# A value sum with 256 columns: four key tiles and 512 queries a period, and the maxima closed at a period's end

## The chip, the cores and the metric

The kernel runs on one core of a Trainium2 chip. The metric is the device time of one execution in microseconds; each kernel is run several times and the median counts. The engines are named as the profile names them: PE (TensorE, with its weight loads as PEld), DVE (VectorE), ACT (ScalarE), POOL (GpSimd) and SP (SyncE, which here only issues DMAs).

## The reference

One token sequence of 2048 rows with 512 columns goes through two branches, softmax attention with 32 heads of 16 columns and a gated feed-forward layer of width 1792, and a sigmoid gate mixes the two:

```
q, k, v = split(x @ wqkv)                      # 32 heads of 16
a = concat_h(softmax(q_h k_h^T / 4) v_h) @ wo
b = (sigmoid(x @ w_gate) * (x @ w_up)) @ w_down
g = sigmoid(sum(x * gate_w))
out = g * a + (1 - g) * b
```

All inputs and the output are fp32.

## The kernel before

**Number formats.** Most products run in a reduced fp32 format (fp32r): a number is split into a high and a low part, and three products are added (`terms`). The value sum (`values`) is plain fp32, and the profile shows two matmul rows for each of its matmuls.

**Stages.** The kernel projects q and k for the first head pairs, then v, while it already computes the first maxima (`first_max`). Then comes the main loop of NPER = 256 periods. Behind it stand the rest of the feed-forward layer and the output product (`whole_run`, `heads_out`).

**A period** handles one step of three works that are interleaved by hand:

- *t*, exponentials (`st_part`, L457): a matmul gives 128 keys x 512 queries of the logits of one head; the 64 rows it contracts hold q and k parts and the row maximum to subtract. ACT takes the exponential into a tile `p` (L470). There are eight a period: two key tiles, two blocks of 512 queries, two heads. Head 0 of two periods runs in an even period, head 1 of two in an odd one.
- *m*, maxima (`sm_step`, L242): for a head pair that comes later, a matmul gives 128 queries x 512 keys (L255) and DVE reduces each row to its maximum (L257). There are eight a period as well.
- *d*, dense (`dense`, class `Sum`): half matmuls (64 contracted rows) of the q, k, gate and up projections, 12 a period. A run of 24 fills bank `dn` in two periods; ACT evicts it (L317).

Head 0's matmuls and the dense half `d0` use the lower 64 rows of the array, head 1's and `d1` the upper. Neighbouring words of the two halves run at once, so the 28 matmuls stand in 14 pairs. At the end of the period `values(k)` (L475) multiplies the exponentials with v: eight matmuls of 512 columns, in which four blocks of 17 output rows (two heads, two query blocks) lie side by side in the array's columns. ACT evicts the sum (L487), and POOL adds it to the sum over the earlier key tiles (L498); after eight periods the sum goes to DRAM (`pv_d`).

**What sets the order.** `STEADY` (L540) lists the words t, m and d of an even and an odd period. Each engine executes its own list strictly in the program's order. Three things limit PE: the array, the banks and the semaphores. Of eight PSUM banks `dn` belongs to the dense work; the other seven go to t, m and the value sum. The table `REUSE` (L542) says for each of the 34 takes of two periods how many takes ago its bank was last taken; that user's reader (ACT for a t or a value sum, DVE for an m) must be done first. Worked through the table, the value sum takes the bank of the period's fifth m in both kinds of period, and the last m that of the fifth t. The last ten periods (`LAST`) have no m.

**Closing the maxima.** When a head has all 32 maxima of 1024 queries, DVE reduces them to eight columns at once (L261). `split_max` (L265) splits these on POOL; two m words later (`DELAY`) `turn_max` (L271) transposes them on DVE (L275), and SP writes them to DRAM and copies them into the rows of `QS` that the t matmuls of that half read (L276, L280). In the steady stage both heads of a pair close in the same odd period, once in eight periods; the first t that needs a half comes two periods or more after.

`turn` (L154) is a token on POOL between the dense halves, behind an even period's words. `logits` (L452) computes the gate's logits on DVE in 16 of the periods.

Of the kernel before, what the change touches and what calls it, by code (L numbers as in the profile page):

```python
# [12 lines left out]
F32 = mybir.dt.float32  # L13
# [12 lines left out]
P = 128  # L26
# [8 lines left out]
KR = 64  # L35
# [2 lines left out]
NSTEP = NPAIR * 32  # L38
NPER = NSTEP // 2
TAIL = FIRST // 2  # L40
DELAY = 2
LOW, UP = 0, 1


# [1 line left out]
def gated_mix(ctx, tc, x, xc, wqk, wv, wo, w_gu, w_down, gate_w, out):  # L46
# [25 lines left out]
    pv_d = dram.tile([2, NPAIR, P, 512], F32, name="pv_d")  # L72
    rec_d = dram.tile([P, 512], F32, name="rec_d")
    m_d = dram.tile([NPAIR, 2, 2, P, 32], F32, name="m_d")

    warm = keep.tile([P, 1], F32, name="warm")
    dve.memset(warm, 0.0)
# [143 lines left out]
    square = ring(keep, 2, [P, 2, 16], "mhl")  # L221
# [13 lines left out]
    xr.update((c, load_x(c)) for c in range(1, NC))  # L235

    stat = {}
    mrow = {}

    count = {}  # L240

    def sm_step(j):  # L242

        p, s = divmod(j, 32)
        qt, kh = divmod(s, 2)
        qs, ks = QS[p % 2], KS[p % 2]

        def one(b, i):
            half = (p, qt // 8, b)
            if half not in stat:  # L250
# [4 lines left out]
            pe.matmul(t, qs[r:r + KM, qt * P:(qt + 1) * P], ks[r:r + KM, g * 512:(g + 1) * 512],  # L255
                      start=True, stop=True)
            dve.tensor_reduce(stat[half][:, qt % 8, g:g + 1], t, axis=AX.X, op=ALU.max)  # L257
            count[half] += 1
            if count[half] == 32:
                m = keep.tile([P, 8], F32, name=f"m{p}_{qt // 8}_{b}", tag="m", bufs=2)  # L260
                dve.tensor_reduce(m, stat.pop(half), axis=AX.X, op=ALU.max)  # L261
                mrow[half] = m
        return one

    def split_max(half):  # L265
        hl = square()
        split(hl[:, 0, :8].bitcast(F32R), hl[:, 1, :8].bitcast(F32R), mrow.pop(half), pool, pool)
        left = iter(range(DELAY))
        turning.append((lambda: next(left, None) is None, half, hl))

    def turn_max():  # L271
        _, half, hl = turning.pop(0)
        p, i, b = half
        mt = keep.tile([P, 32], F32, name=f"mt{p}_{i}_{b}", tag="mt", bufs=2)
        dve.transpose(mt, hl.rearrange("p a t -> p (a t)"))  # L275
        sp.dma_start(m_d[p, i, b], mt)  # L276
        rows = m_d[p, i, b].rearrange("(g a t) j -> a t g j", g=4, a=2)
# [5 lines left out]
    turning = []  # L283

    wd = []

# [31 lines left out]
    fill = filling()  # L318


    first = [(j, i) for j in [*range(0, 16, 2), *range(1, 16, 2), *range(16, FIRST + 1)] for i in range(2)]

    def first_max():
        if first:
            j, i = first.pop(0)
            if j < FIRST:
                sm_step(j)(0, i)
                sm_step(j)(1, i)
            else:
                for j in range(FIRST, FIRST + 2):  # L330
                    sm_step(j)(1, i)

    for c in range(NC):
        if c + 1 < NC:
# [34 lines left out]
    for t in range(2, NS, 2):  # L369
        two = [Sum(bankv(), tokens(t + a)) for a in range(2)]  # L370
        for g in (LOW, UP):
            first_max()
            for m in range(3 * KT):
                two[0].half(g)
                two[1].half(1 - g)
                if m in (5, 11):
                    first_max()
                if turning and turning[0][0]():
                    turn_max()
                for half in list(mrow):  # L380
                    split_max(half)
# [57 lines left out]

    def denominators(i):  # L440
        rows = slice(64 * i, 64 * i + 64)
        sp.dma_start(den[rows, :], pv_d[i].rearrange("p (c r) q -> (p c) r q", r=32)[:, DH, :])
        dve.reciprocal(den[rows, :], den[rows, :])
        sp.dma_start(rec_d[rows, :], den[rows, :])

# [10 lines left out]

    def st_part(k, b):  # L457

        p, r = divmod(2 * k, 32)
        i, kt = divmod(r, 16)  # L460
        qs, ks = QS[p % 2], KS[p % 2]
        r = 64 * b
        pt = ptile[k, b] = mid(f"p{k}_{b}")
        for a in range(2):
            for c in range(2):
                o = bank()
                q0 = i * 1024 + c * 512
                pe.matmul(o, ks[r:r + KR, (kt + a) * P:(kt + a + 1) * P], qs[r:r + KR, q0:q0 + 512],  # L468
                          start=True, stop=True)
                act.activation(pt[:, 2 * a + c, :], o, AF.Exp, scale=DH ** -0.5)  # L470
                yield

    sums = {}

    def values(k):  # L475

        o = bank()
        half = divmod(k // 8, 2)
        pts = [ptile.pop((k, b)) for b in range(2)]
        for a in range(2):  # L480
            for c in reversed(range(4)):
                h = 2 * half[0] + c // 2
                pe.matmul(o[32 * c:32 * c + VW, :], v[:, 2 * k % 16 + a, h * VW:(h + 1) * VW],  # L483
                          pts[c // 2][:, 2 * a + c % 2, :], start=(a == 0), stop=(a == 1))

        def put(e):
            act.activation(e, o, AF.Copy)  # L487

        if half not in sums:
            sums[half] = keep.tile([P, 512], F32, name=f"sum{half[0]}_{half[1]}", tag="sum", bufs=2)  # L490
            put(sums[half])
        else:
            e = keep.tile([P, 512], F32, name=f"part{k}", tag="part", bufs=2)
            put(e)
            later.append(lambda s=sums[half]: add(s, e))

        def add(s, e):
            pool.tensor_tensor(s, s, e, ALU.add)  # L498
            if k % 8 == 7:
                sp.dma_start(pv_d[half[1], half[0]], s)  # L500

    def mx(b):
        for j in range(FIRST + 2 * b, NSTEP):
            one = sm_step(j)
            for i in range(2):
                one(b, i)
                yield
# [17 lines left out]
    def emit(order, **parts):  # L525

        for word in order.split():
            if word == "turn":
                turn(run)
            elif word == "work":  # L530
                work(1)
            else:
                next(parts[word], None)
                if word[0] == "m":
                    if turning and turning[0][0]():
                        turn_max()
                    for half in list(mrow):
                        split_max(half)

    STEADY = ("t0 m1 d1 m0 t0 d1 d1 m0 t0 d1 t0 d1 d1 m0 d1 work m0 t0 d1 t0 d1 d1 t0 m1 t0 d1 m0 d1 m0",  # L540
              "t1 m0 t1 d0 d0 m1 t1 d0 d0 m1 d0 m1 t1 d0 work m1 d0 t1 d0 d0 t1 m1 m0 t1 d0 d0 t1 d0 m1")
    REUSE = (7, 5, 8, 6, 9, 7, 7, 6, 8, 6, 8, 6, 8, 7, 7, 6, 8,  # L542
             7, 7, 7, 7, 7, 7, 7, 6, 8, 7, 7, 7, 7, 6, 8, 6, 8)
# [13 lines left out]
    for k in range(NPER):  # L557
# [6 lines left out]
        if 128 <= n < 256 and n % 16 in (6, 8):  # L564
            logits((n - 128) // 16 * 2, (n % 16 - 6) // 2)
        if n % 32 == 0 and n // 32 + 1 < NPAIR:
            load_pair(n // 32 + 1)
        if k >= NPER - TAIL:
# [5 lines left out]
        if k >= NPER - TAIL and turning:  # L574
            turn_max()
        emit(STEADY[k % 2] if k < NPER - TAIL else LAST[k - NPER], **parts)
        if k == NPER - 1:
            bankd = bank
        if run.done():
# [49 lines left out]
                raws.append(late_raw(*late[1][:2]))  # L629

    def heads_load(u):
        i, c, q0 = u // 4, (u // 2) % 2, (u % 2) * 256
        ot = lp.tile([P, KT, 256], F32, name=f"ot{u}", tag="ot")
        rb = lp.tile([P, KT, 256], F32, name=f"rb{u}", tag="rb")
        heads = pv_d[i].rearrange("p (b c r) q -> (p b) c r q", b=2, c=2)
        recs = rec_d.rearrange("(i h c) q -> i h c q", i=2, c=2)
        for k in range(KT):
            hs = slice(8 * k, 8 * k + 8)
            sp.dma_start(ot[:, k, :], heads[hs, c, :DH, q0:q0 + 256])
            sp.dma_start(rb[:, k, :], recs[i, hs, c, q0:q0 + 256].unsqueeze(1).to_broadcast([8, DH, 256]))  # L640
        return ot, rb

    def heads_split(u, ot, rb):
# [89 lines left out]
```

## Time and profile before

| What | Value |
|---|---|
| median of the runs | 1758.79 us (1758.29 to 1759.24, 3 runs) |
| the profiled execution's own time | 1758.72 us |
| its span | 1756.2 us |
| PE, PEld | 1749.5 us (100%), 1060.2 us (60%) |
| DVE, ACT, POOL | 1422.0 us (81%), 1321.8 us (75%), 478.1 us (27%) |
| main loop, first to last steady period | 96.8 to about 1473 us |
| its last ten periods | about 1473 to 1523 us |
| granted clock of PE | 0.998 |

A row of the timeline gives the start in us from the span's start, the duration in us, the engine, the line, the operation, what it writes and reads, and how many equal rows were merged; in square brackets stands the idle time ahead of it and what ended it. `sm` and `st` are the seven shared banks. A row of the groups gives the total busy time and the mean of one in ns. In the table of windows each engine's busy time is followed by its count.

### The profile page before, as it was taken

The numbers are of one execution on the slowest core, as the hardware profiler recorded it, in microseconds if no ns is written. First come the engines' busy times: TensorE is split into PE (matmuls) and PEld (weight loads), VectorE is DVE, ScalarE is ACT, GpSimd is POOL, SyncE is SP. The second block draws the span as 40 slices with busy tenths as digits, with TensorE's granted clock in tenths as the row PEclk, the third lists the DMA queues.
The fourth block names the chain that finished last, engine by engine and source line by source line (L and its number), as shares of the span: only waits on it lengthen the run. The fifth ranks groups of instructions, "written<-read, shape, count | busy, mean of one in ns | idle before, by whom it ended". The sixth has DMA issues, their size and how long they took to land.

```text
span 1756.2 us, 33183 instructions
## 1 busy us (share of the span) xinstructions
PE 1749.5 (100%) x12676; PEld 1060.2 (60%) x12676; DVE 1422.0 (81%) x2346; ACT 1321.8 (75%) x2564; POOL 478.1 (27%) x501
## 2 busy tenths in 40 slices
PE   9999999999999999999999999999999999999999
PEld 7755555555555555555555555555555555588887
DVE  5988888888998889888888888888888886256543
ACT  4188888888888888888888888888888888944221
POOL 1124343423232313222222222222222222342110
PEclk9999999999999999999999999999999999999999
DMA  9311424241313131413131313122121312367652
GB/s 254 78 37 61 88 68 92 68 104 44 80 56 80 48 75 47 85 51 86 38 74 38 74 36 65 45 59 53 50 63 44 63 44 68 120 227 256 232 191 72
DMA packets 89567, 149.75 MB, mean 85 GB/s; under 512 B 23424, under 2 KB 31616, under 8 KB 86400
## 3 DMA queue, kind: packets, MB, share of 16 engines
q1 hardware_dynamic: 89120, 147.11, 31.2%
q8 instruction: 99, 1.62, 0.4%
q14 instruction: 60, 0.49, 0.1%
q10 hardware_dynamic: 288, 0.52, 0.1%
HBM read 87.56 MB, written 60.03 MB: 84 GB/s over the span
## 4 chain that ended last, share of the span: by engine, by line
PE 99%; DVE 0%; ACT 0%; issue 0%
PE dn L145 19%; PE sm L483 16%; PE sm L468 12%; PE st L483 11%; PE sm L255 10%; PE st L468 9%; PE sm L688 7%; PE st L255 7%; PE st L132 4%; PE dn L688 2%; PE st L145 1%; PE sm L597 1%; PE st L597 1%; PE st L80 0%; DVE stat L257 0%; ACT p L470 0%
## 5 line engine op out<-in xcount | busy, mean ns | idle before, releaser
L257 DVE TENSOR_REDUCE stat<-sm 128x1 f32<-128x512 f32 x1205 | 774.2, 680 | 100.3 <-PE sm L255 87.4
L470 ACT ACTIVATE p<-sm 128x512 f32<-128x512 f32 x1167 | 666.9, 652 | 0.1
L257 DVE TENSOR_REDUCE stat<-st 128x1 f32<-128x512 f32 x843 | 552.0, 679 | 70.9 <-PE st L255 61.9
L470 ACT ACTIVATE p<-st 128x512 f32<-128x512 f32 x881 | 522.2, 652 | 9.2 <-PE st L468 8.6
L498 POOL TENSOR_TENSOR sum<-sum,part 128x512 f32<-128x512 f32 x224 | 289.3, 1291 | 722.8 <-ACT part L487 696.6
L255 PE MATMUL sm<-ks,qs 48*128 48x512 f32 x1205 | 463.7, 419 | 0.2 <-DVE stat L257 0.2
L468 PE MATMUL sm<-qs,ks 64*128 64x512 f32 x1167 | 454.6, 424 | 0.3 <-ACT part L487 0.3
L468 PE MATMUL st<-qs,ks 64*128 64x512 f32 x881 | 351.6, 425 | 1.5 <-ACT v L361 1.4
L255 PE MATMUL st<-ks,qs 48*128 48x512 f32 x843 | 341.8, 419 | 0.0
L468 PEld LDWEIGHTS sm<-qs,ks 64*128 64x128 f32 x1167 | 211.2, 185 | 174.6 <-ACT gu L317 48.5
L483 PE MATMUL sm<-p,v 128*17 128x512 f32 x2384 | 285.1, 595 | 0.0
L255 PEld LDWEIGHTS sm<-ks,qs 48*128 48x128 f32 x1205 | 218.3, 185 | 38.1 <-DVE stat L257 7.8
L468 PEld LDWEIGHTS st<-qs,ks 64*128 64x128 f32 x881 | 161.1, 186 | 130.9 <-ACT gu L317 35.7
L483 PE MATMUL st<-p,v 128*17 128x512 f32 x1712 | 204.6, 595 | 0.0
L255 PEld LDWEIGHTS st<-ks,qs 48*128 48x128 f32 x843 | 155.4, 185 | 25.0 <-DVE stat L257 3.0
L487 ACT ACTIVATE part<-sm 128x512 f32<-128x512 f32 x132 | 81.1, 614 | 107.8 <-issue 92.7
L483 PEld LDWEIGHTS sm<-p,v 128*17 128x17 f32 x2384 | 55.4, 96 | 141.1 <-issue 92.2
L487 ACT ACTIVATE part<-st 128x512 f32<-128x512 f32 x92 | 56.2, 611 | 77.7 <-issue 62.9
L483 PEld LDWEIGHTS st<-p,v 128*17 128x17 f32 x1712 | 39.7, 96 | 100.9 <-issue 66.2
L96 POOL CAST mhl<-m 128x8 fp32r<-128x8 f32 x64 | 12.1, 189 | 272.7 <-DVE m L261 272.7
L432 DVE TENSOR_TENSOR gul<-gul 128x1024 f32<-128x1024 f32 (+1 forms) x30 | 45.9, 1536 | 34.6 <-ACT gul L431 33.4
L317 ACT ACTIVATE gu<-dn 128x512 f32<-128x512 f32 x99 | 69.1, 698 | 0.0
(456 smaller groups left out, 3042.9 us busy)
## 6 DMA issues: line engine op xcount, KB each, us to landing
gu_d<-gu SPq DMA_DIRECT2D x112, 256.0 KB
gul<-gu_d SPq DMA_DIRECT2D x56, 512.0 KB
qs<-q_d SPq DMA_DIRECT2D x90, 128.0 KB
ks<-k_d SPq DMA_DIRECT2D x90, 128.0 KB
pv_d<-sum SPq DMA_DIRECT2D x32, 256.0 KB
q_d<-qe SPq DMA_DIRECT2D x12, 512.0 KB
k_d<-qe SPq DMA_DIRECT2D x12, 512.0 KB
x<-in_xc_dram SPq DMA_DIRECT2D x16, 256.0 KB
```

The lines of the kernel that those rows point to most:

```text
L132: pe.matmul(o, a, b, start=(i == 0), stop=(i == len(ops) - 1))
L145: mm = pe.matmul(self.o, a[rows], b[rows], start=(self.n == 0), stop=(self.n == 2 * len(self.ops) - 1))
L255: pe.matmul(t, qs[r:r + KM, qt * P:(qt + 1) * P], ks[r:r + KM, g * 512:(g + 1) * 512], start=True, stop=True)
L257: dve.tensor_reduce(stat[half][:, qt % 8, g:g + 1], t, axis=AX.X, op=ALU.max)
L317: leave = lambda e, o: act.activation(e, o, AF.Copy)
L432: dve.tensor_tensor(gu[:, 1, a], gu[:, 0, a], gu[:, 1, a], ALU.mult)
L468: pe.matmul(o, ks[r:r + KR, (kt + a) * P:(kt + a + 1) * P], qs[r:r + KR, q0:q0 + 512], start=True, stop=True)
L470: act.activation(pt[:, 2 * a + c, :], o, AF.Exp, scale=DH ** -0.5)
L483: pe.matmul(o[32 * c:32 * c + VW, :], v[:, 2 * k % 16 + a, h * VW:(h + 1) * VW], pts[c // 2][:, 2 * a + c % 2, :], start=(a == 0), stop=(a ...
L487: act.activation(e, o, AF.Copy)
L498: pool.tensor_tensor(s, s, e, ALU.add)
L688: pe.matmul(down[t], a, b, start=(f == 0 and m == 0), stop=(f == NF - 2 and m == 5))
```

## The change

A period now takes four key tiles and 512 queries in place of two key tiles and 1024 queries. It still has eight t, eight m and 12 d words. What changes:

- `values` issues 16 matmuls of 256 columns: four key tiles, two heads, two halves of the 512 queries. Its output has 256 columns in a bank, so the eviction on ACT and the addition on POOL have 256 columns too. A sum is complete after four periods, with three additions; there are 64 sums of half the size, and the layout of `pv_d` and its readers (`denominators`, `heads_load`) follow.
- `STEADY` and `REUSE` are new tables.
- The closing of the maxima moves behind the words of a period: reduce (now L268), transpose (L270) on DVE, then the split on POOL, which now works on the transposed tile of 32 columns, then the DMAs. `DELAY` and `split_max` go.
- Head 1's maxima run 24 steps ahead in place of 22 (`UPPER`); the additional ones are computed in the first stage. The heads now close in two different odd periods of eight.
- The gate's logits stand behind a period's words too, before its value sum.

```diff
-DELAY = 2
+UPPER = FIRST + 4
...
             if count[half] == 32:
-                m = keep.tile([P, 8], F32, name=f"m{p}_{qt // 8}_{b}", tag="m", bufs=2)
-                dve.tensor_reduce(m, stat.pop(half), axis=AX.X, op=ALU.max)
-                mrow[half] = m
+                full.append(half)
...
     def turn_max():
-        _, half, hl = turning.pop(0)
+        half = full.pop(0)
         p, i, b = half
+        m = square()
+        dve.tensor_reduce(m[:, :8], stat.pop(half), axis=AX.X, op=ALU.max)
         mt = keep.tile([P, 32], F32, name=f"mt{p}_{i}_{b}", tag="mt", bufs=2)
-        dve.transpose(mt, hl.rearrange("p a t -> p (a t)"))
-        sp.dma_start(m_d[p, i, b], mt)
+        dve.transpose(mt, m)
+        hl = keep.tile([P, 2, 32], F32R, name=f"mhl{p}_{i}_{b}", tag="mhl", bufs=2)
+        split(hl[:, 0, :], hl[:, 1, :], mt, pool, pool)
+        sp.dma_start(m_d[p, i, b], hl.bitcast(F32))
...
-        for a in range(2):
-            for c in reversed(range(4)):
-                h = 2 * half[0] + c // 2
-                pe.matmul(o[32 * c:32 * c + VW, :], v[:, 2 * k % 16 + a, h * VW:(h + 1) * VW],
-                          pts[c // 2][:, 2 * a + c % 2, :], start=(a == 0), stop=(a == 1))
+        for a in range(4):
+            for b in reversed(range(2)):
+                h = 2 * p + b
+                for i in reversed(range(2)):
+                    r = 64 * b + 32 * i
+                    pe.matmul(o[r:r + VW, :], v[:, 4 * k % 16 + a, h * VW:(h + 1) * VW],
+                              pts[b][:, a, 256 * i:256 * i + 256], start=(a == 0), stop=(a == 3))
...
-    REUSE = (7, 5, 8, 6, 9, 7, 7, 6, 8, 6, 8, 6, 8, 7, 7, 6, 8,
+    REUSE = (8, 7, 7, 7, 7, 7, 7, 6, 8, 7, 7, 7, 6, 8, 6, 8, 7,
...
         emit(STEADY[k % 2] if k < NPER - TAIL else LAST[k - NPER], **parts)
+        while full:
+            turn_max()
+        if 128 <= n < 256 and n % 16 in (4, 8):
+            logits((n - 128) // 16 * 2, (n % 16 - 4) // 4)
```

Two places show what this makes of the engines' lists. The first is PE at the end of an even period and the start of its value sum. Line L255 (now L254) is an m, L468 (now L461) a t, L145 a d, L483 (now L478) the value sum; `waits` names the semaphores that the row waits for. Before:

```order
L468 MATMUL sm_70<-qs_106,ks_107 128x512 [waits DVE_49]
L255 MATMUL st_66<-ks_107,qs_106 128x512 [waits Activation_49]
L255 MATMUL sm_69<-ks_107,qs_106 128x512 [waits DVE_49]
L468 MATMUL sm_71<-qs_106,ks_107 128x512 [waits Activation_49]
L145 MATMUL dn<-xh,g5h 128x512
L145 MATMUL dn<-xl,g5h 128x512
L468 MATMUL st_67<-qs_106,ks_107 128x512 [waits DVE_49]
L145 MATMUL dn<-xh,g5l 128x512
L255 MATMUL st_65<-ks_107,qs_106 128x512 [waits Activation_49]
L483 MATMUL sm_72<-p_1_9198,v 17x512 [waits DVE_49]
```

In the kernel after the change, the same place:

```order
L254 MATMUL st_67<-ks_107,qs_106 128x512 [waits DVE_49]
L145 MATMUL dn<-xl,u5h 128x512
L145 MATMUL dn<-xh,u5l 128x512
L254 MATMUL sm_71<-ks_107,qs_106 128x512 [waits Activation_49]
L461 MATMUL st_67<-qs_106,ks_107 128x512 [waits DVE_49]
L254 MATMUL sm_70<-ks_107,qs_106 128x512 [waits Activation_49]
L478 MATMUL sm_72<-p_1_10262,v 17x256 [waits Activation_49]
L478 MATMUL sm_72<-p_1_10262,v 17x256
L478 MATMUL sm_72<-p_0_10311,v 17x256 x2
L478 MATMUL sm_72<-p_1_10262,v 17x256 x2
```

The value sum waited for a reduce on DVE and now waits for ACT: by the new table it takes the bank of the period's sixth t, in both kinds of period. The last m still waits for the fifth t, and the last t of an even period, beside it, for the fourth m. The order of the last words differs: four m in place of three now stand among the last six users of a bank.

The second place is DVE around the closing of one pair's maxima. L257 (now L256) is the reduce of a matmul's row maxima, L261 (now L268) the closing reduce, L275 (now L270) the transpose. Before:

```order
L257 TENSOR_REDUCE stat_1_1_3873<-st_66 128x1 [waits PE_49]
L261 TENSOR_REDUCE m_1_1_4382<-stat_1_1_3873 128x8 [waits DVE_49]
L257 TENSOR_REDUCE stat_0_1_4387<-sm_71 128x1 [waits PE_49]
L257 TENSOR_REDUCE stat_0_1_4387<-sm_69 128x1 [waits PE_49]
L257 TENSOR_REDUCE stat_0_1_4387<-st_67 128x1 [waits PE_49]
L275 STREAM_TRANSPOSE mt_1_1_4406<-mhl_117 128x32 [waits DMAHW1_49,Pool_49]
L257 TENSOR_REDUCE stat_1_0_3934<-st_66 128x1 [waits PE_49]
L261 TENSOR_REDUCE m_1_0_4413<-stat_1_0_3934 128x8 [waits DVE_49]
```

After the change, around the closing of one head:

```order
L256 TENSOR_REDUCE stat_1_0_4317<-st_65 128x1 [waits PE_49]
L256 TENSOR_REDUCE stat_0_1_4740<-st_66 128x1 [waits PE_49]
L268 TENSOR_REDUCE msq_118<-stat_1_0_4317 128x8 [waits DVE_49]
L270 STREAM_TRANSPOSE mt_1_0_4855<-msq_118 128x32 [waits DVE_49,Pool_49]
L256 TENSOR_REDUCE stat_0_1_4740<-st_67 128x1 [waits PE_49]
```

The closing reduce and the transpose stood apart, between reduces of matmuls of the same period, with the split on POOL between them. Now they stand together behind the last reduce of a period and ahead of the first of the next, and the split comes after them.

More of the change, by code (lines that the diff above doesn't have):

```diff
@@ L220, in gated_mix @@
     act.activation(g1[:, :1], warm, AF.Exp)
-    square = ring(keep, 2, [P, 2, 16], "mhl")
+    square = ring(keep, 2, [P, 32], "msq")
     for _ in range(2):
@@ L318, in gated_mix @@
     fill = filling()
[L321 removed]
+    first = [(j, i) for j in [*range(0, 16, 2), *range(1, 16, 2), *range(16, FIRST), *range(FIRST, UPPER, 2)] for i in range(2)]
     def first_max():
@@ L463, in st_part @@
         pt = ptile[k, b] = mid(f"p{k}_{b}")
-        for a in range(2):
[L465 to L471, printed above, removed]
+        for a in range(4):
+            o = bank()
+            pe.matmul(o, ks[r:r + KR, (kt + a) * P:(kt + a + 1) * P], qs[r:r + KR, c * 512:(c + 1) * 512],
+                      start=True, stop=True)
+            act.activation(pt[:, a, :], o, AF.Exp, scale=DH ** -0.5)
+            yield
@@ L473, in gated_mix @@
     sums = {}
     def values(k):
-        o = bank()
-        half = divmod(k // 8, 2)
+        o = bank()[:, :256]
+        p, c = part = divmod(k // 4, 4)
         pts = [ptile.pop((k, b)) for b in range(2)]
-        for a in range(2):
-            for c in reversed(range(4)):
-                h = 2 * half[0] + c // 2
-                pe.matmul(o[32 * c:32 * c + VW, :], v[:, 2 * k % 16 + a, h * VW:(h + 1) * VW],
-                          pts[c // 2][:, 2 * a + c % 2, :], start=(a == 0), stop=(a == 1))
@@ L486, in put @@
[L486 to L495, printed above, removed]
+        for a in range(4):
+            for b in reversed(range(2)):
[4 more added lines that the diff above has]
+                              pts[b][:, a, 256 * i:256 * i + 256], start=(a == 0), stop=(a == 3))
@@ L497, in add @@
+        if part not in sums:
+            sums[part] = keep.tile([P, 256], F32, name=f"sum{p}_{c}", tag="sum", bufs=2)
+            act.activation(sums[part], o, AF.Copy)
+        else:
+            e = keep.tile([P, 256], F32, name=f"part{k}", tag="part", bufs=2)
+            act.activation(e, o, AF.Copy)
+            later.append(lambda s=sums[part]: add(s, e))
         def add(s, e):
             pool.tensor_tensor(s, s, e, ALU.add)
-            if k % 8 == 7:
-                sp.dma_start(pv_d[half[1], half[0]], s)
+            if k % 4 == 3:
+                sp.dma_start(pv_d[c, p], s)
@@ L502, in mx @@
     def mx(b):
-        for j in range(FIRST + 2 * b, NSTEP):
+        for j in range(UPPER if b else FIRST, NSTEP):
             one = sm_step(j)
```

59 lines of the change are left out of this document (23 added, 36 removed).

## Prediction

> **What bounds the kernel now.** The page comes first: TensorE is busy for the whole span, and the chain that ended last runs through it alone.
>
> ```profile
> span 1756.2 us, 33183 instructions
> PE 1749.5 (100%) x12676; PEld 1060.2 (60%) x12676; DVE 1422.0 (81%) x2346; ACT 1321.8 (75%) x2564; POOL 478.1 (27%) x501
> ...
> PE 99%; DVE 0%; ACT 0%; issue 0%
> ```
>
> That does not say that matrix work is the limit: ends of matmuls are modelled, and a matmul that started late counts as busy. The starts decide. I take the start of a period's value sum (V below, L483) as the mark; the critical chain in order of time shows one cycle of eight periods (a head pair has four lists of maxima, two to a cycle):
>
> ```profile
> 904.50 1.84 PE sm L483 x16
> 910.11 1.84 PE sm L483 x16
> ...
> 932.53 1.84 PE st L483 x16
> 938.36 1.84 PE st L483 x16
> 944.06 1.84 PE sm L483 x16
> 949.67 1.39 PE sm L483 x9
> ```
>
> A plain period takes 5.61 us. The two around the closing of the maxima take 5.83 and 5.70, 0.32 more together; the cycle is 949.67 - 904.50 = 45.17. There are 246 steady periods, so 245 steps from V to V, 30.6 cycles.
>
> Next the timeline of one plain period. TensorE:
>
> ```profile
> 904.43 1.91 PE L483 MATMUL sm<-p,v 128*17 128x512 f32 x16
> 906.27 0.49 PE L468 MATMUL sm<-qs,ks 64*128 64x512 f32 x1
> 906.61 0.39 PE L255 MATMUL st<-ks,qs 48*128 48x512 f32 x1
> 906.84 0.39 PE L468 MATMUL st<-qs,ks 64*128 64x512 f32 x1
> ...
> 909.71 0.39 PE L255 MATMUL st<-ks,qs 48*128 48x512 f32 x1
> 910.04 0.62 PE L483 MATMUL sm<-p,v 128*17 128x512 f32 x4
> ```
>
> V holds the array 1.84 us (904.43 to 906.27). Then 14 pairs of half-array matmuls follow: 0.34 to the second, 0.23 from pair to pair, and 0.33 from the last to V. Unhindered that is 0.34 + 12 x 0.231 + 0.33 = 3.44, so V would come at 906.27 + 3.44 = 909.71. It comes at 910.04: 0.33 us of each period are waits. The weight loads and ScalarE say for whom:
>
> ```profile
> 904.43 0.13 PEld L483 LDWEIGHTS sm<-p,v 128*17 128x17 f32 x8 [0.30 <-DVE stat L257]
> 904.87 0.12 PEld L483 LDWEIGHTS sm<-p,v 128*17 128x17 f32 x4 [0.31 <-issue]
> 905.30 0.12 PEld L483 LDWEIGHTS sm<-p,v 128*17 128x17 f32 x4 [0.31 <-issue]
> ...
> 906.61 0.19 PEld L468 LDWEIGHTS st<-qs,ks 64*128 64x128 f32 x1
> ...
> 909.56 0.18 PEld L255 LDWEIGHTS st<-ks,qs 48*128 48x128 f32 x1
> ```
>
> ```profile
> 905.16 0.70 ACT L317 ACTIVATE gu<-dn 128x512 f32<-128x512 f32 x1
> 906.46 0.60 ACT L487 ACTIVATE part<-sm 128x512 f32<-128x512 f32 x1 [0.60 <-issue]
> 906.95 0.59 ACT L470 ACTIVATE p<-sm 128x512 f32<-128x512 f32 x1
> 907.43 1.09 ACT L470 ACTIVATE p<-st 128x512 f32<-128x512 f32 x2
> 908.38 0.63 ACT L470 ACTIVATE p<-sm 128x512 f32<-128x512 f32 x1
> 908.86 1.62 ACT L470 ACTIVATE p<-st 128x512 f32<-128x512 f32 x3
> ```
>
> ScalarE has no gap from the eviction at 906.46 on. Its first exponential ends at 907.54, its seventh at 910.48: one each 0.49. The fifth ends at 907.54 + 4 x 0.49 = 909.50. The period's last maximum takes the bank of that fifth exponential (the bank table says so), its weights load at 909.56, 0.05 later, its matmul starts at 909.71, and V 0.33 after that. So the ring is: V's matmuls, eviction, five exponentials, last pair, V. VectorE is the rival that comes close:
>
> ```profile
> 905.43 0.68 DVE L257 TENSOR_REDUCE stat<-st 128x1 f32<-128x512 f32 x1
> 906.84 0.69 DVE L257 TENSOR_REDUCE stat<-sm 128x1 f32<-128x512 f32 x1 [0.74 <-PE sm L255]
> 907.45 0.68 DVE L257 TENSOR_REDUCE stat<-st 128x1 f32<-128x512 f32 x1
> 908.05 2.47 DVE L257 TENSOR_REDUCE stat<-sm 128x1 f32<-128x512 f32 x4
> ```
>
> One reduce each 0.60; the fifth, whose bank V takes, ends at 906.84 + 4 x 0.60 + 0.69 = 909.93, only 0.11 ahead of V. It then idles 0.74 while V runs. The maxima's closing sits in the middle of that row of reduces:
>
> ```profile
> 936.79 0.19 DVE L261 TENSOR_REDUCE m<-stat 128x8 f32<-128x32 f32 x1
> 936.89 1.28 DVE L257 TENSOR_REDUCE stat<-st 128x1 f32<-128x512 f32 x2
> ...
> 941.91 0.20 DVE L275 STREAM_TRANSPOSE mt<-mhl 128x32 f32<-128x32 f32 x1
> ```
>
> **The change part by part.** *The eviction.* It goes from 512 to 256 columns. No row has 256; two sizes bracket its slope:
>
> ```profile
> L431 ACT ACTIVATE gul<-gul 128x1024 f32<-128x1024 f32 x26 | 27.3, 1050 | 8.2 <-DMA gul<-gu_d 8.1
> ...
> L487 ACT ACTIVATE sum<-sm 128x512 f32<-128x512 f32 x17 | 10.2, 598 | 18.8 <-PE sm L483 18.8
> ```
>
> 512 more columns cost 452 ns, so 256 fewer save about 226; between half its slot (0.25 left) and none saved (0.49 left) I take 0.27. ScalarE is then free at 906.46 + 0.27 = 906.73. The first exponential's matmul started at 906.27 and takes 0.49; VectorE, which was idle, began 0.08 after such an end (906.84). So the first exponential starts at 906.84 in place of 906.95, 0.11 earlier; what is late next is its own matmul, and more saving than that is worth nothing here.
>
> *Banks.* V now takes the bank of the sixth exponential, in both kinds of period, and the last maximum still that of the fifth. The sixth ends at 907.43 + 5 x 0.49 = 909.88; with 0.05 to the load V can start at 909.93. By the last pair: fifth end 909.39, load 909.44, matmul 909.59, V 909.92. The two agree within 0.01. VectorE is now asked for its fourth reduce (906.84 + 3 x 0.60 + 0.69 = 909.33), 0.06 ahead of the exponential. The other banks of the new table are free before their pair by the same cadences; the tightest, the seventh maximum on the fourth's bank, is that fourth reduce. V to V: 909.93 - 904.43 = 5.50.
>
> *The value sum.* Eight matmuls of 512 columns become 16 of 256: the same columns through the array, but eight groups of four in place of four. A group now starts each 0.43 (904.43, 904.87, 905.30), so half is 0.215. Dearest neighbour: a pair of the other stage passes 512 columns in one pass in 0.231 and loads 128 columns of weights (0.19 at 906.61, against 0.12 for four loads here), so at most 8 x (0.231 - 0.215) = 0.13 more. Its loads are nearest to V's own, which hide, so I take 0.005, within the rounding of 5.50, and keep 0.13 for the range. That PE can issue twice as many rows shows in the first load row: eight, done after 0.13, began within 0.03, if one takes 0.10 (its row stands at the third rival).
>
> Here the Trainium skill speaks against the change: "TensorE: Matmul & The Clock Gate", section "Part 3: Packing small matmuls — row/col tiling", says that weight loads overlap running matmuls only where the row groups differ, and V's matmuls all use every row. The rows above disagree: the loads at 904.87 begin with the group that runs until 905.30, and the next group is not late. By the rule the sum would gain the third rival's term below; I go by the rows.
>
> *Closing the maxima.* Reduce, transpose and split now follow a period's last maximum. They cost VectorE 0.19 + 0.20 there, in the idle time ahead of the next period's first reduce. With 5.50 that idle time is 0.74 - 0.11 = 0.63, so the 0.32 per cycle go. If the cover is too short they come back, at most 0.32 x 30.6 = 10 us. GpSimd's split, on 32 columns, follows there; the period's end is odd, where no token for TensorE stands behind it. SyncE's row transfers start earlier than now (941.91 was 3.6 us after a V, the new place is about 2.2), so they are due no sooner than they can land. GpSimd's shorter additions and SyncE's 32 further stores lie beside 27% and are worth nothing.
>
> *The logits* stay in that idle time:
>
> ```profile
> 471.13 0.68 DVE L454 CUSTOM_DVE_ANT_0 xn<-xn,gwb 128x512 f32<-128x512 f32 x1
> 471.74 0.08 DVE L454 DVE_READ_ACCUMULATOR2_ANT logit<- 128x1 f32 x1
> 471.95 0.69 DVE L257 TENSOR_REDUCE stat<-sm 128x1 f32<-128x512 f32 x1
> ```
>
> From 471.13 to the next reduce at 471.95 is 0.82, against 0.63: 0.2 late, less 0.06 of slack, 16 times: +2.2.
>
> *Ends.* Four maxima for the second head move from the steady stage to the start: 4 x 0.60 = 2.4 at most, I take +1.2; the two last steady periods lose them, -0.6. The ten periods behind have no maxima and hang on ScalarE:
>
> ```profile
> 1473.30:1523.40 50.10, 49.76 (x359) 23.73 (x356) 10.92 (x17) 48.43 (x100) 14.56 (x16) 1.00 0.11 34
> ```
>
> ScalarE (fourth figure, 48.43 of 50.10) saves 10 x 0.22 = 2.2 there. The stage after it is untouched.
>
> *Sum.* A cycle takes 8 x 5.50 = 44.00, 1.17 less; 30.6 x 1.17 = 35.8. In all -35.8 + 2.2 + 1.2 - 0.6 - 2.2 = -35.2. The profiled execution took 1758.72 (its span and 2.5 around it), the runs' median is 1758.79, so no correction: 1758.7 - 35.2 = 1723.5.
>
> **The rivals.** *First: the shorter eviction brings nothing.* The first exponential stays at 906.95, the sixth ends at 907.54 + 5 x 0.49 = 909.99, V comes at 910.04 as now, and only the closing's 0.32 x 30.6 = 10 are won: 1749. For it: nothing here shows 256 columns. Against: the slope above.
>
> *Second: the short groups cost what a pair costs.* V is 0.13 longer, a period 5.63, a cycle 45.04: -4 on the steady stage, 1754. It needs a fixed cost per group that the 0.43 spacing does not show.
>
> *Third, the other side: the added weight loads stand in the open.* The page's groups give one load:
>
> ```profile
> L483 PEld LDWEIGHTS sm<-p,v 128*17 128x17 f32 x2384 | 55.4, 96 | 141.1 <-issue 92.2
> ```
>
> Four further groups, each with a load of 96 ns ahead of it, add 0.39 to V and so to the ring, which starts with it: 5.89 a period, 47.1 a cycle, +1.95 x 30.6 = +60, 1818. It turns slower once V grows by more than 0.14 + 0.01, the gain per period. Its chance is low because the same loads hide today behind groups twice as long; at 0.12 against 0.215 they still fit. (It is what the Trainium skill's rule on row groups, named above, would do here.)
>
> *Fourth: the wait goes altogether.* If ScalarE, started sooner, does its exponentials at the spacing of their starts, or the waits shift, V comes at matrix pace, 909.71: 5.28 a period, 42.2 a cycle, 1758.7 - 91 = 1668.
>
> *Fifth: the closing is not hidden.* Then 1733.
>
> **How the numbers follow.** Forecast 62%, 1723.5. First rival 12%, second 10%, third 8%, fourth 3%, fifth 5%. The range leaves out the third, the fourth and the dearer half of the second, 16 to 18 of 100: up to 1753 for the first rival and a second one in part. Downward, exponentials at their starts' spacing (0.477 from 906.95, 907.43) would save 5 x 0.013 = 0.07 a period, 16 us: 1707, rounded to 1705. Within 0.2% means within 3.5 us, about what a measurement can tell here. Faster: forecast, first, fourth and fifth (82%) and a little of the second, 83%; same 7%, most of the second; slower 10%.
>
> **What would show it.** Right: V to V near 5.50, all eight alike; the eviction about 0.37 long and the first exponential 0.57 after the first pair's start in place of 0.68; V's row still about 1.9 with groups 0.215 apart; reduce and transpose of the maxima ahead of the idle gap, not between reduces. Wrong: groups wider than 0.23, a period of 5.6 with an early first exponential (then another bank is late, and the load before V names it), or VectorE's idle gap gone.

## The result and the profile after

The changed kernel takes 2370.2 us (median of 4 runs, 2369.2 to 2373.4), before 1758.7 (1758.3 to 1759.2): ratio 1.348, interval 1.3457 to 1.3503. That is 611 us slower where 35 faster was forecast. The profiled execution has a span of 2368.3. Its page, first the totals and then the chain that ended last:

```profile
span 2368.3 us, 41683 instructions
...
PE 1925.2 (81%) x16772; PEld 1142.8 (48%) x16772; DVE 1495.0 (63%) x2346; ACT 1345.2 (57%) x2564; POOL 331.7 (14%) x469
...
PE 55%; DVE 34%; ACT 9%; issue 2%; ACTq 0%
```

Before, TensorE was busy for 100% of the span and carried 99% of the chain. Now every engine stands part of the time, and a third of the chain runs through VectorE: engines that wait for each other in turn, not one engine at its limit. The critical chain in order of time shows where, by the starts of the value sum V (now L478):

```profile
908.30 1.91 PE st L478 x32
...
916.36 1.85 PE sm L478 x32
...
924.36 1.90 PE st L478 x32
...
932.40 1.90 PE sm L478 x32
...
940.41 1.90 PE st L478 x32
```

A period takes 8.00 to 8.06 (8.15 as a mean over the 245 steps, since 21 of them take 9.5 to 9.7), before 5.65. That is 245 x 2.51 = 614: the whole loss lies in the steady stage. V itself has not grown: behind an even period the next pair starts 1.85 after it, before 1.84. (Behind an odd one it starts 2.49 after it, but that is a wait, shown below.) The 21 long steps are those in which the granted clock drops. The table of windows shows one of them and the step behind it; the clock is the third figure from the end:

```profile
147.79:157.30 9.51, 7.59 (x63) 3.80 (x61) 4.22 (x7) 4.45 (x9) 0.72 (x1) 0.84 0.01 2
157.30:165.33 8.03, 6.40 (x63) 3.64 (x61) 5.96 (x10) 5.26 (x11) 3.17 (x4) 1.00 0.21 65
```

Together they cost about 33 us of the 611; before, the clock was 1.00 throughout the steady stage. Why it drops no run isolates, but it is a small part of the loss. The groups by line say which tiles the waits stand at. First the two rows of the maxima's reduces before, then those rows after, with four rows of weight loads:

```profile
L257 DVE TENSOR_REDUCE stat<-sm 128x1 f32<-128x512 f32 x1205 | 774.2, 680 | 100.3 <-PE sm L255 87.4
...
L257 DVE TENSOR_REDUCE stat<-st 128x1 f32<-128x512 f32 x843 | 552.0, 679 | 70.9 <-PE st L255 61.9
```

```profile
L256 DVE TENSOR_REDUCE stat<-st 128x1 f32<-128x512 f32 x1262 | 832.2, 687 | 468.7 <-PE dn L145 189.5
...
L256 DVE TENSOR_REDUCE stat<-sm 128x1 f32<-128x512 f32 x786 | 531.9, 685 | 243.2 <-PE sm L254 104.4
...
L254 PEld LDWEIGHTS st<-ks,qs 48*128 48x128 f32 x1262 | 219.1, 184 | 483.9 <-DVE stat L256 169.6
...
L461 PEld LDWEIGHTS st<-qs,ks 64*128 64x128 f32 x1024 | 180.5, 186 | 337.4 <-DVE stat L256 315.8
...
L461 PEld LDWEIGHTS sm<-qs,ks 64*128 64x128 f32 x1024 | 184.2, 186 | 19.9 <-issue 2.5
...
L254 PEld LDWEIGHTS sm<-ks,qs 48*128 48x128 f32 x786 | 143.3, 185 | 56.8 <-issue 39.9
```

`sm` are four banks and `st` three. The same 2048 maxima now use the `st` banks 1262 times, before 843 times, and the loads of m and t wait there: 484 and 337 us ahead of `st` tiles, 57 and 20 us ahead of `sm` tiles. Worked through from its start, the table says why: in the steady periods `st_67` is taken in five of a period's 17 takes (m, t and V), and `sm_69` in none. The timeline of one odd period shows what that does; the last figure of a row in brackets is idle time and what ended it:

```profile
905.31 0.39 PE L254 MATMUL st<-ks,qs 48*128 48x512 f32 x1
905.54 1.28 DVE L256 TENSOR_REDUCE stat<-st 128x1 f32<-128x512 f32 x2
...
906.87 0.18 PEld L461 LDWEIGHTS st<-qs,ks 64*128 64x128 f32 x1 [1.61 <-DVE stat L256]
906.88 0.50 PE L461 MATMUL st<-qs,ks 64*128 64x512 f32 x1 [1.18 <-DVE stat L256]
...
908.24 1.43 PEld L478 LDWEIGHTS st<-p,v 128*17 128x17 f32 x32 [0.37 <-ACT p L463]
...
910.29 0.38 ACT L486 ACTIVATE part<-st 128x256 f32<-128x256 f32 x1 [0.81 <-PE st L478]
910.72 0.18 PEld L254 LDWEIGHTS st<-ks,qs 48*128 48x128 f32 x1 [1.06 <-ACT part L486]
...
911.26 1.97 DVE L256 TENSOR_REDUCE stat<-st 128x1 f32<-128x512 f32 x3 [0.96 <-PE sm L461]
```

At 905.31 an m is put into `st_67`. The very next take, a t, goes into the same bank and so waits for the reduce of that m: the second of the two reduces from 905.54 on ends at 906.82, the load starts at 906.87. Two takes that are 0.23 apart elsewhere are 1.57 apart here. At 908.24 V takes `st_67` too, and the first m of the next period takes it again: it waits until V's eviction ends at 910.67. So one bank now has five users in a period, each of which must come behind the reader of the one before it, and where two of them stand close together TensorE waits.

The cause is one number. `REUSE` says how many takes back the bank is looked up, in a history that starts as the seven banks listed twice. The new table starts with 8 (the old one with 7): the first take gets the bank of eight back, the last of the first list, `st_67`, while `st_67` also stands last in the second list, ready for a later 7. From there on the table only hands banks on from place to place: seven places, but `st_67` in two of them and `sm_69` in none.

What the prediction said one would see of the edits themselves is there: the eviction of 256 columns takes 384 ns (the median), V's 32 rows start in groups of four 216 ns apart, and the closing stands ahead of the idle gap.

### The profile page after: what moved, and what is told of

It reads as the page before. It is cut to its first block, busy times and chain, and to the rows that moved or that the text cites. A ratio compares the mean times of both kernels' runs of the same rounds, so it can differ in the third digit from the quotient of the medians.

```text
span 2368.3 us, 41683 instructions
## 1 busy us (share of the span) xinstructions
PE 1925.2 (81%) x16772; PEld 1142.8 (48%) x16772; DVE 1495.0 (63%) x2346; ACT 1345.2 (57%) x2564; POOL 331.7 (14%) x469
## 4 chain that ended last, share of the span: by engine, by line
PE 55%; DVE 34%; ACT 9%; issue 2%; ACTq 0%
DVE stat L256 34%; PE st L478 14%; PE st L254 10%; PE sm L478 8%; ACT p L463 6%; PE st L461 6%; PE sm L676 5%; ACT part L486 3%; PE st L132 3%; PE sm L254 2%; PE sm L461 2%; PE dn L145 2%; PE dn L676 1%; PE st L145 1%; PE sm L584 1%
## 5 line engine op out<-in xcount | busy, mean ns | idle before, releaser
L256 DVE TENSOR_REDUCE stat<-st 128x1 f32<-128x512 f32 x1262 | 832.2, 687 | 468.7 <-PE dn L145 189.5
L254 PE MATMUL st<-ks,qs 48*128 48x512 f32 x1262 | 533.4, 445 | 222.0 <-ACT p L463 90.6
L463 ACT ACTIVATE p<-sm 128x512 f32<-128x512 f32 x1024 | 573.6, 607 | 224.9 <-PE sm L461 202.9
L256 DVE TENSOR_REDUCE stat<-sm 128x1 f32<-128x512 f32 x786 | 531.9, 685 | 243.2 <-PE sm L254 104.4
L461 PE MATMUL st<-qs,ks 64*128 64x512 f32 x1024 | 412.1, 432 | 214.1 <-DVE stat L256 210.6
L254 PEld LDWEIGHTS st<-ks,qs 48*128 48x128 f32 x1262 | 219.1, 184 | 483.9 <-DVE stat L256 169.6
L461 PE MATMUL sm<-qs,ks 64*128 64x512 f32 x1024 | 385.5, 406 | 0.0
L461 PEld LDWEIGHTS st<-qs,ks 64*128 64x128 f32 x1024 | 180.5, 186 | 337.4 <-DVE stat L256 315.8
L478 PE MATMUL st<-p,v 128*17 128x256 f32 x5376 | 334.3, 391 | 0.8 <-DVE stat L256 0.8
L254 PE MATMUL sm<-ks,qs 48*128 48x512 f32 x786 | 322.3, 424 | 1.2 <-DVE stat L256 0.7
L490 POOL TENSOR_TENSOR sum<-sum,part 128x256 f32<-128x256 f32 x192 | 140.3, 731 | 1028.2 <-ACT part L486 907.9
L478 PEld LDWEIGHTS st<-p,v 128*17 128x17 f32 x5376 | 144.4, 99 | 162.5 <-ACT p L463 46.1
L461 PEld LDWEIGHTS sm<-qs,ks 64*128 64x128 f32 x1024 | 184.2, 186 | 19.9 <-issue 2.5
L478 PE MATMUL sm<-p,v 128*17 128x256 f32 x2816 | 191.3, 418 | 0.0
L254 PEld LDWEIGHTS sm<-ks,qs 48*128 48x128 f32 x786 | 143.3, 185 | 56.8 <-issue 39.9
L478 PEld LDWEIGHTS sm<-p,v 128*17 128x17 f32 x2816 | 79.3, 104 | 87.3 <-issue 42.0
```

The costliest lines, as they stand in the source:

```text
L463: act.activation(pt[:, a, :], o, AF.Exp, scale=DH ** -0.5)
L478: pe.matmul(o[r:r + VW, :], v[:, 4 * k % 16 + a, h * VW:(h + 1) * VW], pts[b][:, a, 256 * i:256 * i + 256], start=(a == 0), stop=(a == 3))
```

## The experiments

Nine kernels are edits of the changed kernel and three are edits of before.

**The history seeded.** One more entry makes the first 8 find the bank that 7 would have found, so that the seven places hold seven banks; nothing else differs from the changed kernel.

```diff
-    given = [*seven, *seven]
+    given = [*seven, *seven, seven[1]]
```

> The kernel after the change, with one more entry in the history of banks ahead of the main loop, so that the table's first entry (eight takes back) finds a bank of its own. Theory A (one bank stands for two of the seven places and another for none; the rest of the plan holds): 1723, between 1705 and 1753, all seven banks in use, V to V near 5.50. Theory B (the plan itself is at fault: the value sum waits for ScalarE's sixth exponential, and the new order of words makes chains of waits): still above 2000.

Measured: 1724.4 (1723.9 to 1724.6), before on the same chip 1757.8 (1756.4 to 1759.7); ratio 0.9812, interval 0.9797 to 0.9827. One entry is worth 646 us. V to V, from the critical chain in order of time:

```profile
898.80 1.91 PE sm L478 x32
...
904.32 1.91 PE st L478 x32
...
909.84 1.91 PE sm L478 x32
...
915.36 1.92 PE st L478 x32
...
920.87 1.92 PE sm L478 x32
...
926.39 1.92 PE sm L478 x32
...
931.91 1.92 PE sm L478 x32
...
937.43 1.91 PE st L478 x32
...
942.94 1.92 PE sm L478 x32
```

All these steps are 5.51 or 5.52, closing periods included; the mean of all 245 is 5.52. The granted clock is 1.00 throughout. The timeline of the period that starts at 904.31:

```profile
904.31 1.92 PE L478 MATMUL st<-p,v 128*17 128x256 f32 x32
...
906.17 0.49 PE L461 MATMUL st<-qs,ks 64*128 64x512 f32 x1
...
906.36 0.38 ACT L486 ACTIVATE part<-st 128x256 f32<-128x256 f32 x1 [1.12 <-PE st L478]
...
906.73 0.60 ACT L463 ACTIVATE p<-st 128x512 f32<-128x512 f32 x1
...
908.66 1.61 ACT L463 ACTIVATE p<-sm 128x512 f32<-128x512 f32 x3
...
909.24 0.18 PEld L254 LDWEIGHTS st<-ks,qs 48*128 48x128 f32 x1 [0.20 <-DVE stat L256]
...
909.70 1.28 DVE L256 TENSOR_REDUCE stat<-st 128x1 f32<-128x512 f32 x2
909.83 1.21 PEld L478 LDWEIGHTS sm<-p,v 128*17 128x17 f32 x28 [0.31 <-ACT p L463]
```

It is the forecast's ring: the eviction 0.38 long, the first exponential 0.56 after its pair (906.17 to 906.73), the fifth to seventh from 908.66 with the last ending at 910.27, so the sixth at 910.27 - 0.49 = 909.78; V's loads start 0.05 later and name an exponential, as they do in 244 of the 246 steady periods. The load at 909.24 belongs to the last pair and names a reduce, the fourth; it is in time.

**The same fault put into before.** The history of before gets `st_67` in two places and loses `sm_69`.

```diff
-    given = [*seven, *seven]
+    given = [*seven, seven[6], *seven[1:]]
```

> The kernel before, with the same fault put into its history: the first of the seven places gets the last bank's number, so one bank serves two places and one none. Theory A: far slower, 2100 to 2500, with waits of TensorE on the doubled bank in the middle of each period. Theory B: little changes, 1759 to 1850, as the old order of words is sound.

Measured: 2326.0 (one run), 568 us above before, with a mean steady period of 7.96. The fault needs nothing of the change: with it, the old words, table, value sum and closing lose about as much by it.

**The 256-column sum alone, in before**, with the old words, table and closing:

```diff
-        o = bank()
+        o = bank()[:, :256]
...
-        for a in range(2):
-            for c in reversed(range(4)):
...
+        for a in range(4):
+            for b in reversed(range(2)):
+                h = 2 * p + b
+                for i in reversed(range(2)):
```

> The kernel before, with four key tiles and 256 columns in the value sum alone (old order of words, old table, old closing). By the prediction's ring the first exponential comes 0.11 us earlier, V is then held by the fifth reduce (909.93 + 0.05): 5.55 a period, 13 us less, 1745. If the shorter eviction brings nothing: 1759. If the added weight loads stand in the open: 1850.

Measured: 1759.9 (1758.8 to 1760.9), ratio 1.0012 (1.0003 to 1.0022). The gain that I expected is missing. The timeline, one period (V is L485 here, an m L255, a t L468):

```profile
906.18 1.92 PE L485 MATMUL sm<-p,v 128*17 128x256 f32 x32
...
908.03 0.50 PE L468 MATMUL sm<-qs,ks 64*128 64x512 f32 x1
...
908.57 0.60 ACT L470 ACTIVATE p<-sm 128x512 f32<-128x512 f32 x1
908.60 0.69 DVE L257 TENSOR_REDUCE stat<-sm 128x1 f32<-128x512 f32 x1 [0.74 <-PE sm L255]
...
909.81 2.47 DVE L257 TENSOR_REDUCE stat<-sm 128x1 f32<-128x512 f32 x4
...
911.14 0.18 PEld L255 LDWEIGHTS sm<-ks,qs 48*128 48x128 f32 x1 [0.27 <-DVE stat L257]
911.14 0.50 PE L255 MATMUL sm<-ks,qs 48*128 48x512 f32 x1
...
911.48 0.39 PE L255 MATMUL st<-ks,qs 48*128 48x512 f32 x1
911.80 0.13 PEld L485 LDWEIGHTS sm<-p,v 128*17 128x17 f32 x8 [0.37 <-DVE stat L257]
```

The exponentials do come earlier: the first starts 0.54 after its pair, before 0.68. But the last m but one waits for the fourth reduce (909.81 + 0.60 + 0.68 = 911.09, load at 911.14), the last m follows 0.34 behind it, and V 0.32 behind that; 911.80 - 906.18 = 5.62, before 5.61. In before the same two rows of the last m but one stand in the period that the prediction quotes:

```profile
909.38 0.18 PEld L255 LDWEIGHTS sm<-ks,qs 48*128 48x128 f32 x1
909.40 0.47 PE L255 MATMUL sm<-ks,qs 48*128 48x512 f32 x1
```

There the fourth reduce ended at 906.84 + 3 x 0.60 + 0.69 = 909.33 and the load started 0.05 later; the last m came 0.31 behind that matmul (909.71) and V 0.33 behind it (910.04). So before stood on two rings that ended together, one through ScalarE and one through VectorE. The prediction saw the first, and VectorE only in the fifth reduce, 0.11 ahead; shortening one ring alone is worth nothing.

**The closing alone, in before**: reduce, transpose and split behind a period's words, the rest as before.

```diff
-                if word[0] == "m":
-                    if turning and turning[0][0]():
-                        turn_max()
...
+        while full:
+            turn_max()
```

> The kernel before, with the maxima closed behind a period's words alone. Both heads close in one period, two reduces and two transposes, about 0.75 us in an idle time of 0.74: the 0.32 us of a cycle go, 1749. If the idle time does not cover them: 1752 to 1759.

Measured: 1744.5 (1743.2 to 1746.4), ratio 0.9927 (0.9913 to 0.9942). Nearly all steps from V to V are 5.60 to 5.62, those around the closing too, so it hides in the idle time; the whole edit is worth 13 us. In the profiled executions (1756.2 and 1744.5) 8.7 us of that lie in the 245 steps and 3.3 in the last stage, from the start of the last V on. That stage is shorter by 3.1 to 3.8 us in every run with the new closing than in the three with the old one, and no run isolates why.

**The eviction back at 512 columns**, in the seeded kernel. The sum stays at 256 columns; the other half of what is evicted is not used.

```diff
-        o = bank()[:, :256]
+        o = bank()
...
-            e = keep.tile([P, 256], F32, name=f"part{k}", tag="part", bufs=2)
+            e = keep.tile([P, 512], F32, name=f"part{k}", tag="part", bufs=2)
```

> The seeded kernel, but ScalarE evicts all 512 columns of the value sum's bank (half of them are not part of the sum and are not used). If the ring through ScalarE holds it: the first exponential starts 0.10 us later, V to V 5.62, 245 times 0.10 = 25 us more, 1749. If the shorter eviction is worth nothing, as the form alone suggested: 1724.

Measured: 1750.2 (1749.8 to 1750.7), ratio 0.9953 (0.9938 to 0.9968); a period of 5.62. With the new words the eviction is on the ring: 26 us for it.

**The old value sum under the new words, table and closing** (two key tiles, 512 columns), with the seeded history:

```diff
-        for a in range(4):
-            for b in reversed(range(2)):
-                h = 2 * p + b
-                for i in reversed(range(2)):
...
+        for a in range(2):
+            for c in reversed(range(4)):
```

> The seeded kernel with the old value sum (two key tiles, 1024 queries, 512 columns): new order of words, new table and new closing without the new form. If form and table need each other: about 1747, close to the kernel with the new closing alone (1744.5). If the table alone brings the gain: 1722 to 1726.

Measured: 1749.2 (1748.8 to 1749.4), ratio 0.9946 (0.993 to 0.9963). It is the other half of the finding of the 256-column sum alone: words and table without the short eviction gain less than the closing alone (9 us against 13).

**Six banks, each in one place**, all others as in the seeded kernel. It tells a lost bank from a bank in two places:

```diff
-    given = [*seven, *seven, seven[1]]
+    given = seven[1:] * 2
...
-    REUSE = (8, 7, 7, 7, 7, 7, 7, 6, 8, 7, 7, 7, 6, 8, 6, 8, 7,
...
+    REUSE = (6,)
```

> The seeded kernel on six banks that take turns (each take uses the bank of six takes ago); the seventh is left out, as in the kernel after the change, but no bank serves two places. If two places on one bank are the price: 1780 to 1900. If one bank fewer is the price: 2200 or more.

Measured: 1834.4 (one run), a period of 5.97. The changed kernel also uses six banks, at 2370. A lost bank, where the other six take turns evenly, costs 110 us of the 646; the rest, some 33 us at the lower clock included, comes with the two places.

**A plain rotation of seven banks** with the new words:

```diff
-    REUSE = (8, 7, 7, 7, 7, 7, 7, 6, 8, 7, 7, 7, 6, 8, 6, 8, 7,
...
+    REUSE = (7,)
```

> The seeded kernel on seven banks that simply take turns, with no table. If the table's choices matter: 1735 to 1790, as takes wait for readers that are later than need be. If they don't: 1724.

Measured: 1724.0 (1723.5 to 1724.4), ratio 0.9803 (0.9789 to 0.9818), the same as the seeded kernel. With these words the table's departures from 7 are worth nothing, and without them the fault cannot arise (the history is the two lists of seven, with no further entry). V waits for the fifth reduce here in every odd period (122 of 246 name a reduce, 123 an exponential), and a period still takes 5.52. So the gain does not hang on V taking the sixth exponential's bank.

**Two places on one bank, next to each other and apart**, both in that rotation:

```diff
-    given = [*seven, *seven]
+    given = [seven[6], *seven[1:]] * 2
```

> The rotation of seven places, two neighbouring places filled by the same bank and one bank out of use for good (as many banks and the same table as the next run, only the places differ). Theory (two places on one bank serialise the matmul with the reader of the one before it): neighbours are one take apart, so a reduce or an exponential with its start, some 1.1 us, comes between two takes that were 0.23 or 0.33 apart, 17/7 = 2.4 times a period: between 2150 and 2450. Rival (the lost bank is what costs): as with six banks alone, 1834.

```diff
-    given = [*seven, *seven]
+    given = [seven[i] for i in (1, 2, 6, 3, 4, 5, 6)] * 2
```

> The same with the two places on one bank three and four takes apart. Theory: a take three or four back has its reader done or nearly done more often, so this run lies between six banks in rotation and the run with neighbouring places: 1850 to 2050, at least 200 below that run. Rival (the lost bank or the doubling as such is what costs, wherever it lies): the same time as with neighbouring places, within 2%.

Measured: 2471.6 next to each other, 2148.4 apart (one run each). The distance decides, as the theory had it, and the rival of the lost bank falls. Both lie above the ranges that I gave, by 22 and 98 us: in the first I left the price of the lost bank out, and the second had no sum behind it. Against the period of six banks (5.97) the mean periods are 8.56 and 7.25: 2.58 over 2.43 neighbouring takes is 1.06 each, and 1.27 over 4.86 takes three or four apart is 0.26 each. (Without the 30 steps of the first in which the granted clock drops, its figure is 1.01.) These are averages and no single wait. The changed kernel has, per period, 1.5 neighbouring takes on `st_67` and one that is two apart, for 8.15 - 5.97 = 2.18; by estimate the neighbours at 1.06 are 1.6 of it.

**The old words and table with the new sum and closing** (the old table starts with 7 and needs no further entry), and **the old words with the plain rotation**:

```diff
-    STEADY = ("m1 t0 t0 d1 m0 d1 d1 t0 d1 t0 d1 m0 d1 t0 work d1 m0 d1 t0 d1 m0 d1 t0 m0 d1 d1 m0 t0 m1",
...
+    STEADY = ("t0 m1 d1 m0 t0 d1 d1 m0 t0 d1 t0 d1 d1 m0 d1 work m0 t0 d1 t0 d1 d1 t0 m1 t0 d1 m0 d1 m0",
...
+    REUSE = (7, 5, 8, 6, 9, 7, 7, 6, 8, 6, 8, 6, 8, 7, 7, 6, 8,
```

> The seeded kernel with the order of steps in a period and the table of banks as they were before; the 256-column sum and the closing behind the period stay. Theory (the 256-column form pays only with the order that takes the sixth exponential's bank for the value sum): only the closing's gain is left, 1744 to 1748. Rival (form and closing carry the gain): 1724.

> The kernel with the plain rotation of seven banks and the order of steps in a period as it was before. If the old table held the old order back: 1724, as with the new order. If the order itself carries the gain: 1740 to 1750.

Measured: 1747.9 (1747.3 to 1748.5), ratio 0.9943 (0.9926 to 0.9959), and 1835.8 (1835.3 to 1836.2), ratio 1.0443 (1.0428 to 1.0459). The first is as expected: a period of 5.62, V released by a reduce in 245 of the 246 steady periods. The second fell outside both theories: the old words lose 88 us with a plain rotation. Its timeline:

```profile
902.31 1.29 DVE L256 TENSOR_REDUCE stat<-sm 128x1 f32<-128x512 f32 x2 [1.11 <-PE sm L254]
...
903.52 1.28 DVE L256 TENSOR_REDUCE stat<-st 128x1 f32<-128x512 f32 x2
...
904.85 0.18 PEld L461 LDWEIGHTS st<-qs,ks 64*128 64x128 f32 x1 [0.41 <-DVE stat L256]
```

In mid-period a t is given the bank of an m whose reduce, the period's fourth, ends only at 904.80, and the weight loads stand for 0.41. The old table gave the old words other banks there, so they need it where the new words need none; which of its entries matter wasn't tried, nor whether a third table would bring the old words to 1724.

With the closing behind the period, four kernels make a square:

| | old value sum | 256-column sum |
|---|---|---|
| old words and table | 1744.5 | 1747.9 |
| new words and table | 1749.2 | 1724.4 |

Neither step pays alone (+3 and +5), both together are worth 20. (The corner 1744.5 lacks two small edits that the others have: the four maxima ahead and the logits' place.)

## Why the prediction was wrong

- *The ring before.* Right, but half of it: eviction, five exponentials, last pair. That VectorE's ring, through the fourth reduce and the last m but one, ended with it within hundredths of a us, shows in the 256-column sum alone, which gains nothing. In the sum it did no harm: in the new words the fourth reduce releases the last pair of a period (load at 909.24 in the seeded kernel, V at 909.83), and no longer the last but one.
- *The eviction.* Right: 0.38 for 0.37 forecast, first exponential 0.56 after its pair for 0.57, and 26 us for it in the eviction put back.
- *Banks: the step that failed.* "V now takes the bank of the sixth exponential" holds. "The other banks of the new table are free before their pair by the same cadences" does not: it takes for granted that the seven places of the table hold seven banks. I worked the table by how many takes back each entry reaches, and never ran it from its start. The list of PE's rows quoted with the change had it in plain sight: `st_67` for an m, and four rows on for a t, with `sm_69` nowhere. (The rows of before beside them are the end of an odd period and not of an even one, so they are not the same place.) I read the semaphores in those rows and not the names. What the runs showed in its place: seven places on six banks, `st_67` taken five times a period, and a period of 8.15 for the 5.50 forecast. Only this step parts 1724 from 2370, as the one added entry shows.
- *The value sum.* Right: 1.85 from V to the next pair, before 1.84. The third rival, loads in the open, falls, and so does the second.
- *The closing.* Right: hidden, and the steps are alike; alone it gave 13 us for 10, but 8.7 of them in the steps; the gain in the last stage was not foreseen.
- *The logits.* 2.2 forecast; in the seeded kernel the periods with them are no longer than the others.
- *The sum.* Of the seeded kernel's profiled span against before's (1722.5 - 1756.2 = -33.7): up to the first V +2.0 (forecast +1.2), the 245 steps -30.6 (-35.8, +2.2 and -0.6 make -34.2), the ten periods behind -1.9 (-2.2), the last stage -3.2 (0). (The window of the ten periods, 1473.30 to 1523.40, began a period early, as the last steady V starts at 1479.95; that ScalarE sets them holds.) The periods came out at 5.52, not 5.50. The total is within 1.5 us for a kernel that differs from the changed one by one list entry, but that is partly luck: the steps fell short by 3.6 us, and an unforeseen 3.2 us in the last stage made up for it.
- *The chances.* I gave none to the change doing something other than its table says. The slower rival that I had, 1818, was a price of V; the loss came from an edit that I had counted as free. The number of the first rival, 1749, is close to what the seeded kernel takes with the long eviction (1750.2), so that rival was priced rightly.

## What to carry to other kernels

A table of relative distances is only as good as the state it starts from: run it, and count how many different buffers a period uses before any wait in it is priced. A buffer in two places makes the second of two neighbouring users wait for the reader of the first, about 1.06 us a time here; in a page it showed as idle time on all engines, a chain that alternates, and counts of tiles that have moved. Where a step is released by the later of two engines, look how far behind the other is: an edit that shortened one of two rings of equal length brought nothing here until the order relieved the other.

## What the runs showed of the hardware

- Weight loads of a value sum hide behind groups of half the length: V has 32 rows in place of 16, each with its load, and grew by about 0.01. The Trainium skill, "TensorE: Matmul & The Clock Gate", section "Part 3: Packing small matmuls — row/col tiling", says in its list of what overlaps that loads overlap running matmuls only where row groups differ; the text above that list also allows a load into a background weight buffer. Here the matmuls all use the same rows, so the measurement decides against the first statement taken alone; whether the second is the reason no run shows.
- The second pair of half-array matmuls behind a stand started 0.34 after the first and not 0.23 (911.14 to 911.48 in the 256-column sum alone, 906.27 to 906.61 in before).
- The eviction of 256 columns took 384 ns (the median in the seeded kernel), that of 512 columns 598 (in before): by estimate 0.84 ns a column and about 170 ns fixed.
- The granted clock stayed at 1.00 in the steady stage of the seeded kernel, where TensorE has no long stand. In the changed kernel, where it stands in every period, the clock fell to a mean of 0.82 to 0.84 in 21 of 245 steps, each about 1.6 us longer than the rest.
